# First pass of a fused attention and SwiGLU kernel: another order of weight steps, transposes and loads around the tiles of four head pairs

## The chip, the cores and the metric

The kernel runs on one core of one Trainium2 chip. The metric is the device time of one execution in microseconds (us). TensorE (PE) multiplies, VectorE (DVE), ScalarE (ACT) and GpSimd (POOL) do the elementwise work, SyncE (SP) issues DMAs. Each engine takes its instructions in the order in which the program gives them to it; between engines they wait on semaphores.

## What is computed

```python
scores = q @ k.T / sqrt(64)                    # 8 batches, 8 heads, 576 tokens, head_dim 64
p = exp(scores - rowmax) where scores >= rowmax - tau, else 0
x = (p / p.sum()) @ v                          # heads side by side: 4608 tokens x 512
g, val = x @ w_gate, x @ w_val                 # 512 -> 1536
out = (g * sigmoid(g) * val) @ w_out           # 1536 -> 512
```

q, k and v are float32. The weights arrive as 64-bit floats, and the kernel makes float32 numbers of them itself, out of the upper and the lower 32-bit word of each.

## The kernel before, in words

Heads go in pairs: a pair fills 128 partitions. The **first pass** (about the first 124 us) does batch 0, whose four pairs go by 128-token tiles. Everything behind it, seven more batches with the feed-forward block of the batch before them between, is laid out by a planner with costs of its own (`class Plan`), and is not touched.

The first pass is a loop over eight segments n, and in each over tiles x; `(n, x)` names one turn of the loop. Segments 0 to 3 are pairs 0 to 3 with tiles 0 and 1; segments 4 to 7 are pairs 3, 0, 1, 2 with tiles 2, 3 and 4 (tile 4 is half as tall). A turn gives the engines, in this order:

1. PE: the scores of this tile (L505, L513 for tile 4), for head 0 into one PSUM tile and for head 1 into another. There are two such PSUM tiles in all, so the scores of a head wait until the mask of the tile before has read them.
2. DVE: a maximum for each head (L497). Then the point `maxima`.
3. PE: attention times v of the tile before last (L609, L611), then the transposes of the tile before (L578, L582; L576, L584 from segment 4 on).
4. ACT: threshold and exponential for each head (L528, L529), then the copies of what PE has just made (L614, L585, L592). Then the point `flipped`.
5. DVE: the mask with its row sum for each head (L532), then L534 and L535. Then the point `masked`.
6. ACT: in segments 0 to 3 two small matrices with 1/sum on the diagonal (L548), which the transposes of the next turn multiply by. From segment 4 on ACT and POOL scale the tile itself instead (L542, L540). Then the point `end`.

At the four points a table written by hand, `STEPS`, says what else is issued. Its words:

- `weights 2`: fetch up to two of the 24 weight steps, w0, w1, ... (L344, on SP; 768 KB in two DMAs, from `w_gate` and from `w_val`). There are four landing places in turn; a fetch is left out if its place is still held by a step that has not been joined.
- `split`: ACT takes the upper words (L360); POOL (segments 0 to 3, L362) or ACT (later, L364) takes the lower ones; POOL clamps the upper part (L353). In segments 0 to 3 the clamp is issued with the split; later it is put off until step 5 of a turn, where `clamp_split()` issues whatever is unclamped.
- `shift`: DVE (L383), behind the clamp. `join`: DVE adds the sign (L390), then POOL adds the lower part (L400).
- `prepare`: DVE transposes the next pair's keys and queries (L738, L742). `turn`: DVE transposes a pair's other queries (L797). `scale`: POOL scales queries (L440). `qk`, `rest`, `v`: SP issues the loads of a pair's keys and queries (8 DMAs), of its other queries (4), of its values (4).

From segment 4 on a turn has regular steps besides: behind `maxima` a join; at `flipped` a split and two fetches; behind the masks, after the table's own words, a join if something is shifted, `clamp_split()`, an addition of lower parts, and a shift if a step was split in an earlier turn. There PE also fills in products of the feed-forward block (L625), which need the weights joined; ACT reads them by L640 and L641, DVE by L649, and POOL multiplies at the turn's end (L656).

`STARTS` lists the loads that SP gets ahead of the loop. Lines 750 to 752 prepare the first pair of batch 1, whose loads (`qk` at `(4, 0)`) are 8 DMAs of SP and whose queries POOL scales at `(4, 1)`.

Of the kernel before, what the change touches and what calls it, by code (L numbers as in the profile page):

```python
# [27 lines left out]
class Plan:  # L28
# [94 lines left out]

STARTS = ("weights", "v", "weights", "qk", "weights", "v", "v", "weights")

STEPS = {
    (0, 0, "flipped"): ("qk",),
    (0, 1, "maxima"): ("prepare",),  # L130
    (0, 1, "masked"): ("split",),
    (0, 1, "end"): ("scale",),
    (1, 0, "flipped"): ("split", "shift"),
    (1, 0, "masked"): ("join",),
    (1, 1, "flipped"): ("weights 2", "prepare"),
    (1, 1, "masked"): ("split", "shift"),
    (1, 1, "end"): ("join",),
    (2, 0, "maxima"): ("rest", "weights 2"),
    (2, 0, "flipped"): ("rest",),
    (2, 0, "masked"): ("shift", "scale", "split", "join"),  # L140
    (2, 0, "end"): ("weights 2",),
    (2, 1, "maxima"): ("scale", "prepare", "v", "rest"),
    (2, 1, "flipped"): ("rest", "split"),
    (3, 0, "flipped"): ("shift",),
    (3, 0, "end"): ("join",),
    (3, 1, "maxima"): ("shift", "split", "turn last"),
    (3, 1, "flipped"): ("weights 2", "scale", "prepare"),
    (3, 1, "masked"): ("split",),
    (3, 1, "end"): ("turn", "shift", "scale"),
    (4, 0, "flipped"): ("turn", "qk"),  # L150
    (4, 1, "maxima"): ("scale",),
    (4, 1, "masked"): ("scale",),
    (4, 2, "end"): ("turn",),
# [4 lines left out]
def kernel(  # L158
# [620 lines left out]
    def start(what):  # L779
        if what == "weights":  # L780
            fetch_weights()
        elif what == "v":
            load_v(unloaded.popleft())
        elif what == "qk":
            fetch_qk(unfetched.popleft())
        else:
            rest_load()

    for what in STARTS:
        start(what)  # L790
# [1980 lines left out]
```

## Time and profile before

| what | us |
|---|---|
| median of 3 runs | 1332.68 (1331.83 to 1333.17) |
| the profiled execution | 1332.23 |
| its span, first to last instruction | 1330.4 |
| PE busy in the span | 1320.2 (99%) |
| DVE, ACT, POOL busy | 1092.4, 892.9, 951.1 |
| first pass, start to the first scores of the planned part | 123.54 |
| scores of `(1,0)`, `(1,1)`, `(2,0)`, `(2,1)` begin | 15.24, 20.71, 25.48, 30.74 |
| scores of `(3,0)`, `(3,1)`, `(4,0)`, `(4,1)` begin | 36.04, 41.52, 46.29, 56.44 |

Times in the text are counted from the span's start. A busy PE is not a PE at its peak: matmuls of the two heads use different halves of the array and run beside each other when both may start, and one behind the other when the second must wait.

In rows of the timeline the columns are start, length, engine (SPq is SP's queue, PEld the weight loads), line, operation, what it writes and reads, how many, and in brackets how long the engine sat idle before and what ended it. A row of several instructions runs from the first one's start to the last one's end.

### The profile page before, as it was taken

What the parts mean: (1) busy time and instruction counts of PE and PEld (TensorE: products, weight loads), DVE (VectorE), ACT (ScalarE), POOL (GpSimd) and SP (SyncE); (2) the same over time, 40 slices, a digit from 0 to 9 for tenths busy, and PEclk for the clock granted to TensorE, in tenths of its full rate; (3) what the DMA queues carried; (4) which work ended last, traced back from release to release, by engine and by line L of the source; (5) the groups of instructions that cost most, each with busy time, mean ns of one, the idle gap of its engine ahead of it and who ended that gap; (6) DMA issues with size and microseconds to landing.
All of it is one profiled execution on the core that took longest, in us unless ns stands there. A gap on an engine that the chain in (4) does not pass through costs nothing.

```text
span 1330.4 us, 41756 instructions
## 1 busy us (share of the span) xinstructions
PE 1320.2 (99%) x16294; PEld 1119.1 (84%) x16294; DVE 1092.4 (82%) x2900; ACT 892.9 (67%) x2336; POOL 951.1 (71%) x1137
## 2 busy tenths in 40 slices
PE   8999999999999999999999999999999999999998
PEld 7777777777788878888888888887888889999998
DVE  7799988878887788878888887888788888767986
ACT  6898877677755777787777777777777775444300
POOL 3788597565695979756995779677975798866720
PEclk9999999999999999999999999999999999999999
DMA  8853334456647544656265746655465627465341
GB/s 178 220 180 108 71 81 120 126 155 178 161 168 228 168 152 114 202 157 222 71 203 165 235 107 193 180 166 154 111 202 157 217 74 227 152 208 189 96 171 40
DMA packets 230884, 209.81 MB, mean 158 GB/s; under 512 B 167968, under 2 KB 185376, under 8 KB 223008
## 3 DMA queue, kind: packets, MB, share of 16 engines
q1 hardware_dynamic: 226768, 206.22, 52.4%
q8 instruction: 129, 2.11, 0.7%
q10 hardware_dynamic: 3920, 0.92, 0.3%
q14 instruction: 67, 0.55, 0.1%
HBM read 169.08 MB, written 38.01 MB: 156 GB/s over the span
## 4 chain that ended last, share of the span: by engine, by line
PE 94%; ACT 3%; DMA 1%; POOL 1%; DVE 1%; SPq 1%; issue 0%; ACTq 0%; DVEq 0%
PE pb L1190 14%; PE px L1820 12%; PE sc L2111 10%; PE pa L1190 10%; PE xa L2211 10%; PE pe L1190 6%; PE po L1498 6%; PE sc L2601 5%; PE py L1820 4%; PE pe L1385 3%; PE pb L2601 2%; PE pg L1423 2%; PE pa L2601 2%; PE pv L1423 2%; PE py L1829 2%; PE sc L1820 1%
## 5 line engine op out<-in xcount | busy, mean ns | idle before, releaser
L2159 DVE SCALAR_TENSOR_TENSOR pall<-sc,th,pall 128x288 f32<-128x288 f32 x504 | 244.2, 514 | 39.3 <-ACT pall L2157 20.2
L2157 ACT ACTIVATE pall<-sc,nm 128x288 f32<-128x288 f32 x504 | 232.7, 497 | 34.9 <-DVE pall L2159 34.7
L1190 PE MATMUL pb<-xall,big 128*128 128x256 f32 x864 | 205.9, 381 | 0.0
L2189 DVE STREAM_TRANSPOSE pall<-pall 128x576 f32<-128x576 f32 x252 | 188.4, 764 | 19.2 <-ACT pall L2187 9.4
L971 POOL TENSOR_TENSOR big<-big 128x128 f32<-128x128 f32 (+3 forms) x226 | 167.1, 748 | 43.5 <-ACT big L1325 21.7
L2187 ACT ACTIVATE pall<-pall,ri 128x288 f32<-128x288 f32 x380 | 175.8, 527 | 27.3 <-DVE ri L2175 26.3
L1190 PEld LDWEIGHTS pb<-xall,big 128*128 128x128 f32 x864 | 161.0, 190 | 24.1 <-issue 2.2
L971 POOL TENSOR_TENSOR hall<-hall,tmp 128x512 f32<-128x512 f32 x80 | 102.1, 1278 | 87.9 <-DVE hall L1249 66.9
L2132 DVE TENSOR_REDUCE mx<-sc 128x2 f32<-128x576 f32 x168 | 125.5, 747 | 45.2 <-PE sc L2111 45.1
L2111 PE MATMUL sc<-kT,qT 64*32 64x288 f32 (+1 forms) x5376 | 144.5, 345 | 0.0
L1190 PE MATMUL pa<-xall,big 128*128 128x256 f32 x576 | 137.6, 382 | 0.0
L2111 PEld LDWEIGHTS sc<-kT,qT 64*32 64x32 f32 x5376 | 95.3, 106 | 48.3 <-issue 8.3
L2211 PE MATMUL xa<-pall,vall 64*32 64x288 f32 x4032 | 128.7, 404 | 0.0
L1190 PEld LDWEIGHTS pa<-xall,big 128*128 128x128 f32 x576 | 107.9, 190 | 17.3 <-issue 2.2
L2211 PEld LDWEIGHTS xa<-pall,vall 64*32 64x32 f32 x4032 | 74.0, 107 | 46.9 <-issue 4.0
L2184 POOL TENSOR_SCALAR pall<-pall,ri 128x288 f32<-128x288 f32 x124 | 63.5, 523 | 49.0 <-DVE ri L2175 46.9
L2168 ACT COPY sums<-sums 32x6 f32<-32x6 f32 x336 | 66.6, 198 | 31.3 <-DVE pall L2159 26.2
L1190 PE MATMUL pe<-xall,big 128*128 128x256 f32 x352 | 83.9, 381 | 0.0
L2134 DVE TENSOR_REDUCE mx<-sc 128x1 f32<-128x288 f32 x168 | 75.0, 447 | 0.0
L1190 PEld LDWEIGHTS pe<-xall,big 128*128 128x128 f32 x352 | 66.3, 190 | 10.3 <-ACT xlast L2223 0.7
L971 POOL TENSOR_TENSOR hall<-hall 128x384 f32<-128x384 f32 (+2 forms) x69 | 70.3, 1032 | 0.8
L971 POOL TENSOR_TENSOR big<-hall 128x384 f32<-128x384 f32 (+2 forms) x69 | 65.6, 972 | 4.3 <-PE pa L1190 4.2
(402 smaller groups left out, 3055.7 us busy)
## 6 DMA issues: line engine op xcount, KB each, us to landing
big<-sums_hbm SPq DMA_DIRECT2D x30, 1280.0 KB, 7.6
big<-sums_hbm SPq DMA_DIRECT2D x30, 1024.0 KB, 7.4
vall<-in_v_dram SPq DMA_DIRECT2D x112, 144.0 KB, 4.0
big<-sums_hbm SPq DMA_DIRECT2D x54, 256.0 KB, 3.6
sums_hbm<-big SPq DMA_DIRECT2D x36, 256.0 KB, 3.6
out_dram<-big SPq DMA_DIRECT2D x32, 256.0 KB, 3.1
qT<-in_q_dram SPq DMA_DIRECT2D x112, 72.0 KB, 4.2
kT<-in_k_dram SPq DMA_DIRECT2D x112, 72.0 KB, 3.0
```

The source lines that it names most:

```text
L971: nc.gpsimd.tensor_tensor(out=out, in0=a, in1=b, op=op)
L1190: nc.tensor.matmul(ps[:, i], w[:, k_, i * P:(i + 1) * P], x[:, k_, :], start=first and i == k_ == 0, stop=True, skip_group_check=True)
L1498: nc.tensor.matmul(ps, h(f), w[:, f, :], start=(f == 0), stop=(f == NF2 - 1))
L1820: nc.tensor.matmul(ps, a[:, f, :], ws[n][:, f, :], start=bank_ not in begun, stop=True, skip_group_check=True)
L2111: nc.tensor.matmul(pss[h][(slice(g * G, (g + 1) * G), *part)], qT[hs, col:col + G], kT[hs, c * SH + keys[0]:c * SH + keys[1]], start=True, ...
L2132: rs.append(job("DVE", 0.72, lambda n=n, tile_=tile_: nc.vector.tensor_reduce(out=mx[:, n:n + 2, 0], in_=tile_[:, :, 0:SH], axis=AX.X, op= ...
L2157: ej = job("ACT", 0.42, lambda x=x, n=n: nc.scalar.activation(ps[x], scs[x], AF.Exp, bias=nm[:, n:n + 1]), ej, masks.get((h, u - 1)), rank=0)
L2159: masks[x] = job("DVE", 0.45, lambda x=x, n=n: nc.vector.scalar_tensor_tensor(out=ps[x], in0=scs[x], scalar=th[:, n:n + 1], in1=ps[x], op0 ...
L2187: scaled.append(job("ACT", 0.46, lambda x=x, n=n: nc.scalar.activation(x, x, AF.Copy, scale=ri[:, n:n + 1]), rj, rank=rank))
L2189: seg["turned"].append(job("DVE", 0.72, lambda both=both: nc.vector.transpose(out=both, in_=both), *scaled, rank=rank))
L2211: nc.tensor.matmul(holds[a].ap()[x * G:(x + 1) * G, 0:SH].rearrange("d (i q) -> d i q", q=G), vr[rs, h, j, ds], p[rs, h, :, j, :], start=( ...
L2601: nc.tensor.matmul(both.ap(b_)[:, at_ * P:(at_ + 1) * P], ws[x], xd[x], start=b_ not in begun, stop=True, skip_group_check=True)
```

## The change

Only the two tables differ. Nothing is added to the computation and nothing left out; all 24 weight steps are made.

- `STARTS`: the keys and queries of the fourth pair are loaded behind pair 1's values and ahead of pair 2's; before, they came at `(0, 0)`, behind step w3.
- `prepare` of pairs 2 and 3 goes from in front of the masks of `(1, 1)` and `(2, 1)` to behind the masks of `(1, 0)` and `(2, 0)`.
- Joins: w0 goes from behind the masks of `(1, 0)` to behind those of `(1, 1)`, w1 from the end of `(1, 1)` to behind the masks of `(2, 1)`, w2 from `(2, 0)` to the end of `(3, 0)`. The shifts of w1 and w2 go to `flipped` of `(2, 0)` and `(3, 0)`.
- One split, shift and join fewer by the end of segment 3, where the next step is w6 and not w7. The end of `(4, 0)` makes that up: a join (w5), up to two fetches, a shift (w6) and a split (w7).
- As places come free later, the fetches move too: w4 to the end of `(1, 1)`, w5 to the end of `(2, 1)`, behind the loads `rest`, `v`, `rest`, `rest` of segment 2; w6 to `(3, 1)`; w7 and w8 to `(4, 0)`, w8 behind the 8 DMAs of `qk`.
- The third pair's `scale` (of pair 3's early queries) goes from `(2, 0)` to the end of `(1, 1)`.

From `(4, 1)` on the table is the same, and both orders work on the same weight step.

```diff
-STARTS = ("weights", "v", "weights", "qk", "weights", "v", "v", "weights")
+STARTS = ("weights", "v", "weights", "qk", "weights", "v", "qk", "v", "weights")
 STEPS = {
-    (0, 0, "flipped"): ("qk",),
...
-    (1, 0, "flipped"): ("split", "shift"),
-    (1, 0, "masked"): ("join",),
-    (1, 1, "flipped"): ("weights 2", "prepare"),
-    (1, 1, "masked"): ("split", "shift"),
-    (1, 1, "end"): ("join",),
-    (2, 0, "maxima"): ("rest", "weights 2"),
-    (2, 0, "flipped"): ("rest",),
-    (2, 0, "masked"): ("shift", "scale", "split", "join"),
-    (2, 0, "end"): ("weights 2",),
-    (2, 1, "maxima"): ("scale", "prepare", "v", "rest"),
-    (2, 1, "flipped"): ("rest", "split"),
+    (1, 0, "flipped"): ("split", "shift",),
+    (1, 0, "masked"): ("prepare",),
+    (1, 1, "masked"): ("split", "join",),
+    (1, 1, "end"): ("weights 2", "scale",),
+    (2, 0, "maxima"): ("rest",),
+    (2, 0, "flipped"): ("rest", "shift",),
+    (2, 0, "masked"): ("prepare",),
+    (2, 1, "maxima"): ("scale", "v", "rest",),
+    (2, 1, "flipped"): ("rest", "split",),
+    (2, 1, "masked"): ("join",),
+    (2, 1, "end"): ("weights 2",),
     (3, 0, "flipped"): ("shift",),
     (3, 0, "end"): ("join",),
-    (3, 1, "maxima"): ("shift", "split", "turn last"),
-    (3, 1, "flipped"): ("weights 2", "scale", "prepare"),
+    (3, 1, "maxima"): ("shift", "split", "turn last",),
+    (3, 1, "flipped"): ("weights 2", "scale", "prepare",),
     (3, 1, "masked"): ("split",),
-    (3, 1, "end"): ("turn", "shift", "scale"),
-    (4, 0, "flipped"): ("turn", "qk"),
+    (3, 1, "end"): ("turn", "shift", "scale",),
+    (4, 0, "flipped"): ("turn", "qk",),
+    (4, 0, "end"): ("join", "weights 2", "shift", "split",),
     (4, 1, "maxima"): ("scale",),
     (4, 1, "masked"): ("scale",),
```

## The prediction

> **What bounds the kernel now.** I read the page, then the chain of waits, then a table of stretches for the first pass, then each engine's timeline.
>
> ```profile
> span 1330.4 us, 41756 instructions
> ...
> PE 94%; ACT 3%; DMA 1%; POOL 1%; DVE 1%; SPq 1%; issue 0%; ACTq 0%; DVEq 0%
> ```
>
> PE sets the end nearly everywhere, but the chain's pieces before 124 us also run through ACT, POOL and DVE. All that the change moves lies there, so only that part is worked out; the planned part behind it keeps its order and should begin, and end, later or earlier by the same amount.
>
> One turn each, from its scores to the next scores; columns: length, then busy time of PE, PEld, DVE, ACT, POOL, clock, DMA.
>
> ```profile
> 20.71:25.48 4.77, 4.77 (x48) 3.84 (x46) 4.12 (x8) 4.45 (x12) 3.32 (x3) 1.00 0.80 186
> 25.48:30.74 5.26, 5.26 (x48) 4.24 (x46) 4.83 (x11) 4.28 (x12) 3.44 (x3) 1.00 0.94 208
> ```
>
> The same 48 matmuls take 4.77 or 5.26. The surplus is in the scores: 1.25 when both heads run beside each other, up to 1.95 when the second waits for its PSUM tile, that is, for the mask of the turn before. The turns from 15.24 to 46.29 take 5.47, 4.77, 5.26, 5.30, 5.48, 4.77: above 4.77 they lose 0.70 + 0 + 0.49 + 0.53 + 0.71 + 0 = **2.43 us**. That is all there is to win up to 46.29.
>
> Why the masks are late is in DVE's timeline:
>
> ```profile
> 23.32 0.77 DVE L738 STREAM_TRANSPOSE pall<-extra 128x576 f32<-128x576 f32 x1
> 24.01 0.40 DVE L742 STREAM_TRANSPOSE qT<-extra 128x256 f32<-128x256 f32 x1
> 24.34 0.78 DVE L532 SCALAR_TENSOR_TENSOR pall<-sc,th,pall 128x576 f32<-128x576 f32 x1
> ...
> 26.17 0.54 DVE L383 TENSOR_SCALAR big<-big 128x768 uint32<-128x768 uint32 x1
> 26.75 0.96 DVE L390 SCALAR_TENSOR_TENSOR big<-wo,big 128x768 uint32<-128x768 uint32 x1
> 27.62 1.42 DVE L497 TENSOR_REDUCE nm<-sc 128x1 f32<-128x576 f32 x2
> ```
>
> `prepare` holds DVE for 1.02 (23.32 to 24.34), although the exponential was done at 23.70. A shift and a join behind the masks hold it for 1.45 (26.17 to 27.62). Between L535 and the next maximum DVE has some 1.1 (a maximum starts about 1.27 after its scores), so one of `prepare` (1.02) or join (0.96) fits there, and not join and shift together.
>
> **The change, up to 46.29.** The 0.70 of (1,0) stays: its cause is the `prepare` in front of (0,1)'s masks, which isn't moved. At (1,1) the second exponential ends at 24.51, so the masks can end at about 25.3 in place of 25.85, and the scores at 25.48 go side by side: 0.49 won. At (2,0) a shift (0.47) goes in front of the masks, `prepare` behind: the masks end some 0.1 late. At (2,1) and (3,0) only a join or a shift is left beside the masks; of 0.53 + 0.71 about 0.1 to 0.5 stays, the larger figure if w2's join meets w1's addition on POOL (a join took 0.96 alone and 2.04 at 70.95, beside POOL's gate product). So (4,0) begins 1.2 to 1.6 earlier; I take **1.4**. The moved `prepare` of pair 3 needs its keys by about 31: their loads are issued from 20.7 to about 24 now and land by 29 even at the 4.7 that such loads took. A weight step's work less by then is no gain of its own: it comes back at the end of (4,0), where DVE sits idle for 3.64 before 57.71, ACT for 1.89 before 58.48 and POOL for 2.23 before 60.15. The extra join and shift (0.95 + 0.5 of DVE), the split (0.82 + 0.93 of ACT) and the addition (1.82 of POOL) fit, the last two with little left.
>
> **What eats the gain: w5's landing.**
>
> ```profile
> 42.76 4.35 SPq L436 DMA_DIRECT2D extra<-in_q_dram x8
> ...
> 46.72 0.94 ACT L360 ACTIVATE big<-wo 128x768 f32<-128x768 f32 x1
> 47.55 0.69 ACT L548 ACTIVATE pall<-pall,ri 128x128 f32<-128x128 f32 x2
> ...
> 49.29 1.95 PE L578 MATMUL tp<-pall 128*128 128x128 f32 x16
> ```
>
> SP issues almost without a pause up to 47. The split at (3,1) `masked` is w6 now, issued at 38.56. In the change it is w5, and its fetch stands behind the loads of segment 2, the last of which end at 47.1 today. Take away what w5 and w6 cost SP ahead of them (0.89 + 0.87, and SP's waits of 1.2 and up to 0.9 for `w_val` landings in its waits): w5 is issued at about 43.3. Its second half follows 0.45 later; these took 4.8 to land in the median, all halves 3.2 at least. So w5 is there at 47.0 to 48.9, and I take **47.9**. ACT comes to the split at 46.72 - 1.4 = 45.3 and waits; behind it on ACT stand L548, which the next transposes need, and the exponentials of (4,0). 47.9, plus 0.82 of split, plus 0.4 of the first L548 and some 0.2 of signals, lets PE's transposes start at about 49.3, and now they start at 49.29. **The gain of 1.4 is gone**; it is between 0.9 kept and 1.0 lost at the ends of the landing. On POOL the same landing holds w5's lower part and clamp, and with them `scale` (1,1) and one `turn`: by 50.5, as now.
>
> **What is new: a clamp behind a scale.** At (4,0) w7's split now comes at `end`, after that turn's `clamp_split()`. Its clamp is issued at (4,1) behind `scale` (4,0), and the shift of w7 behind it stands in front of the maximum of (4,2).
>
> ```profile
> 56.48 0.83 POOL L353 TENSOR_SCALAR big<-big 128x768 f32<-128x768 f32 x1
> ...
> 61.88 0.54 DVE L383 TENSOR_SCALAR big<-big 128x768 uint32<-128x768 uint32 x1
> 62.13 0.90 POOL L540 TENSOR_SCALAR pall<-pall,ri 128x576 f32<-128x576 f32 x1 [0.16 <-DVE ri L535]
> 62.33 0.75 DVE L497 TENSOR_REDUCE nm<-sc 128x1 f32<-128x576 f32 x1
> ...
> 63.00 1.55 POOL L440 TENSOR_SCALAR qT<-qT,scl 128x576 f32<-128x576 f32 x1
> ...
> 64.94 0.78 ACT L529 ACTIVATE pall<-sc,nm 128x576 f32<-128x576 f32 x1
> ...
> 73.87 2.06 PE L505 MATMUL sc<-pall 64*128 64x288 f32 x10 [0.85 <-DVE pall L532]
> ```
>
> Today w7's clamp is done at 57.3. Then: POOL's L440 from 63.03. It took 1.55 beside DVE's join; DVE would be waiting, so I take 0.90, L540's time for the same shape: 63.93. Clamp 0.83: 64.8. Shift 0.46, maximum 0.75, threshold 0.25: the exponential of (4,2) starts at 66.25 in place of 64.94, **+1.3** (+1.95 if L440 keeps its 1.55, +1.0 if it takes 0.6). From there the chain of waits has been ACT to 67.68, POOL's clamp of w9, DVE, and PE's scores at 73.87 behind an idle 0.85, with no slack in it, so the 1.3 passes on.
>
> The Trainium skill (SBUF — State Buffer, "SBUF: two separate sides") says that a GpSimd operation and a DVE one with two SBUF inputs exclude each other for a whole instruction. By it the 1.55 of L440 is the join's 0.95 from 63.00, and 0.60 of its own: the sum would be 0.3 lower than mine.
>
> w8 comes behind the 8 DMAs of `qk`, on the place in SP's queue that w9 has now (58.27, less 1.4), and lands at 61.1 to 62.1; ACT asks for it at 61.2. A wait of up to 1.0 there hides in the 1.3, since ACT would otherwise wait for the maximum.
>
> **Sum.** -1.4 won, +1.4 given back to w5, +1.3 for the clamp: **+1.3 us**; 1333.5 on the profiled execution's 1332.23 (span 1330.4 and 1.8 around it). The runs' median is 1332.68, 0.45 above that execution, and a new median is to be compared with it: **1334.0**.
>
> **Rivals.** A measurement of this kernel tells about 0.2% (2.7 us) from no change: faster is below 1330.0, slower above 1335.35.
>
> - *Forecast*, 1334.0 (1333.1 to 1335.0 over the landings above): 0.52.
> - *The gain stays and nothing is given back*: w5 lands by 45.5, since SP's issue alone (0.45 to 0.5 a DMA, 42 from 17.5) would allow it at 39 to 40, and the wait for the clamp finds slack that the chain doesn't show. 1332.68 - 1.4 = 1331.3; at most 2.43, were (1,0) to gain too. For it: the waits that the chain names are inferred. Against it: issues of 1.4 to 2.0 occur in SP's row whenever many loads are out. 0.20, of which 0.04 below 1330.0.
> - *One of the two only*: the gain is eaten, but the clamp's wait is hidden, or the reverse; 1332.7. 0.10.
> - *Slower*: w5 lands much later. Behind the same 8 loads of `rest`, the fetch that follows now took 1.58 to issue its first half (47.28); with that, and the 6.6 that the slowest half took, w5 lands at about 50, ACT holds L548 and the transposes 2.1 longer than I reckon, and the time is 1336.0. It decides above a landing of 49.2. 0.18, of which 0.13 above 1335.35.
>
> Range: 1331.3 to 1335.9, which leaves out about half of the second case and a third of the last. Faster 0.04, within 0.2% 0.82, slower 0.14 (0.13 and the forecast's upper edge).
>
> **What would show it.** Scores of (2,0) and (2,1) of 1.2 to 1.3 and (4,0) starting at 44.7 to 45.1: the front gain. An idle ACT ahead of L360 at 45 to 48, ended by a DMA from `w_val`, and transposes at 49 to 50: w5. DVE idle some 2.9 ahead of L383 near 62, ended by POOL L353: the clamp. Scores of (5,1), now 73.87, near 75.2, and the planned part, now 123.54, near 124.8. It would be wrong if ACT doesn't wait at L360, if L353 of w7 ran before L440, or if the planned part changed its length.

## The result, and the profile after

| | before | after |
|---|---|---|
| median, us | 1332.39 (6 runs, 1331.49 to 1333.17) | 1337.85 (6 runs, 1337.12 to 1339.44) |
| profiled execution, us | 1332.23 | 1338.06 |
| its span, us | 1330.4 | 1336.3 |
| scores of `(3,1)`, `(4,0)`, `(4,1)` begin | 41.52, 46.29, 56.44 | 40.86, 45.63, 57.65 |
| scores of `(4,2)`, `(5,0)`, `(5,1)` begin | 61.03, 66.73, 73.87 | 65.06, 70.77, 79.69 |

The change makes the kernel slower: ratio 1.0041, 95% interval 1.0029 to 1.0054, that is 5.5 us. Forecast were +1.3 us and a range up to 1335.9. (A ratio here and below can differ a little from the quotient of the two medians.)

The profiled execution after starts its first scores 0.22 sooner (6.78 against 7.00). With this as the first step, the way to the 5.82 at the scores of `(5,1)` is: -0.22 of start, -0.44 up to `(4,0)`, +1.87 from there to `(4,1)`, +2.6 at the maximum of `(4,1)`, +2.0 at that of `(4,2)` (the last two counted at the exponentials behind these maxima). The first two places are read from the timeline of after:

```profile
27.49 1.81 POOL L400 TENSOR_TENSOR big<-big,extra 128x768 uint32<-128x768 uint32 x1
27.88 1.85 DVE L383 TENSOR_SCALAR big<-big 128x768 uint32<-128x768 uint32 x1
29.65 0.80 DVE L532 SCALAR_TENSOR_TENSOR pall<-sc,th,pall 128x576 f32<-128x576 f32 x1
...
41.39 4.63 POOL L400 TENSOR_TENSOR big<-big 128x768 uint32<-128x768 uint32 x2
...
44.80 0.42 SPq L344 DMA_DIRECT2D wo<-in_moe_w_val_dram  x1
...
47.98 0.53 POOL L440 TENSOR_SCALAR hall<-hall,scl 128x320 f32<-128x320 f32 x1
48.55 0.51 DVE L797 STREAM_TRANSPOSE pall<-hall 128x320 f32<-128x320 f32 x1 [1.95 <-DMA wo<-in_moe_w_val_dram]
48.78 0.90 ACT L360 ACTIVATE big<-wo 128x768 f32<-128x768 f32 x1 [2.59 <-DMA wo<-in_moe_w_val_dram]
...
50.02 2.05 PE L578 MATMUL tp<-pall 128*128 128x128 f32 x16 [0.91 <-ACT pall L548]
```

w1's shift (L383), in front of the masks of `(2,0)`, takes 1.85; the shift at 61.88 in the kernel before took 0.54. It begins 0.39 after POOL has begun w0's addition (L400) and ends 0.43 after the addition ends at 29.30. The masks (L532), whose exponential was there at 28.3, start at 29.65, and the scores of `(2,1)` run one behind the other (5.47 for the turn, the kernel before 5.30). Then w5: its second half is issued at 44.80, ACT sits idle for 2.59 in front of its split, and PE's transposes of `(4,0)` come at 50.02 and not at 49.29.

Another wait lies beside that one. The maximum of `(4,0)` comes at 50.09, 4.46 after its scores (1.90 in the kernel before, 48.19 after 46.29), and the exponential waits for it until 50.86, though ACT was free again at 50.41. Ahead of the maximum stands the `turn` of pair 0 (L797). Its bracket names a DMA, but it transposes what POOL's `scale` (L440) has written, and starts 0.04 after that ends at 48.51. POOL comes late to this scale because the additions of w1 and w2 fill it until 46.02; they stand behind the `scale` for `(3,1)`, which waited for its queries until 38.86.

The next two places, again in the timeline of after (idle time ahead of an instruction, and what ended it, in the brackets):

```profile
52.44 1.82 POOL L400 TENSOR_TENSOR big<-big,extra 128x768 uint32<-128x768 uint32 x1 [0.97 <-DVE big L390]
54.80 1.68 POOL L540 TENSOR_SCALAR pall<-pall,ri 128x576 f32<-128x576 f32 x1 [0.54 <-PE xa L609]
56.44 2.52 POOL L400 TENSOR_TENSOR big<-big 128x768 uint32<-128x768 uint32 x1
59.06 0.83 POOL L353 TENSOR_SCALAR big<-big 128x768 f32<-128x768 f32 x1
59.85 1.81 POOL L400 TENSOR_TENSOR big<-big 128x768 uint32<-128x768 uint32 x1
59.92 2.15 DVE L383 TENSOR_SCALAR big<-big 128x768 uint32<-128x768 uint32 x1 [2.64 <-POOL big L353]
62.00 1.41 DVE L497 TENSOR_REDUCE nm<-sc 128x1 f32<-128x576 f32 x2
...
67.03 0.75 POOL L440 TENSOR_SCALAR qT<-qT,scl 128x576 f32<-128x576 f32 x1
67.86 1.62 POOL L353 TENSOR_SCALAR big<-big 128x768 f32<-128x768 f32 x2
68.72 1.17 DVE L383 TENSOR_SCALAR big<-big 128x768 uint32<-128x768 uint32 x1 [2.59 <-POOL big L353]
69.82 0.74 DVE L497 TENSOR_REDUCE nm<-sc 128x1 f32<-128x576 f32 x1
```

The upper part is the catch-up at the end of `(4,0)`. Its shift of w6 stands in DVE's row in front of the maximum of `(4,1)`. w6's clamp (59.06) stands in POOL's row behind w3's addition, a scaling of the tile and w4's addition, which fill POOL from 52.44 on but for a pause of 0.54. So DVE waits 2.64 with the scores of `(4,1)` ready since about 58.9, and then the shift itself takes 2.15, beside w5's addition. The maximum (L497) comes at 62.00, 4.35 after the scores of its turn began; in the kernel before it was 1.27 (57.71 after 56.44). The lower part is the second wait, one turn on: w7's clamp behind `scale` (L440), the shift behind the clamp, the maximum of `(4,2)` behind the shift.

From `(5,1)` on nothing more of note is added (5.82 there, 5.9 at the end of the span).

### The profile page after: what moved, and what is told of

The parts are those of the page before. It is cut to its first block, busy times and chain, and to the rows that moved or that the text cites. A ratio compares the mean times of both kernels' runs of the same rounds, so it can differ in the third digit from the quotient of the medians.

```text
span 1336.3 us, 41751 instructions
## 1 busy us (share of the span) xinstructions
PE 1321.0 (99%) x16294; PEld 1119.1 (84%) x16294; DVE 1096.2 (82%) x2900; ACT 894.3 (67%) x2337; POOL 949.5 (71%) x1136
## 4 chain that ended last, share of the span: by engine, by line
PE 92%; ACT 2%; DMA 2%; DVE 1%; POOL 1%; SPq 1%; issue 1%; ACTq 0%; DVEq 0%; POOLq 0%
PE pb L1190 14%; PE px L1820 12%; PE sc L2111 10%; PE pa L1190 10%; PE xa L2211 9%; PE pe L1190 6%; PE po L1498 6%; PE sc L2601 5%; PE py L1820 4%; PE pe L1385 3%; PE pb L2601 2%; PE pg L1423 2%; PE pa L2601 2%; PE pv L1423 2%; PE py L1829 2%; PE sc L1820 1%
## 5 line engine op out<-in xcount | busy, mean ns | idle before, releaser
L971 POOL TENSOR_TENSOR big<-big 128x128 f32<-128x128 f32 (+3 forms) x226 | 167.1, 748 | 43.6 <-ACT big L1325 21.8
```

The lines of the kernel that those rows point to most:

```text
L971: nc.gpsimd.tensor_tensor(out=out, in0=a, in1=b, op=op)
```

## The experiments

The theories. A: the loss comes from the catch-up, whose shifts wait for clamps in front of two maxima and run beside POOL's additions; w5's landing and the shift in front of `(2,0)`'s masks only eat the gain of the front. Its rival puts the loss ahead of `(4,1)`, to w5's landing and to POOL's row of work. All times below are medians; a ratio is against the kernel before, run beside it.

**The catch-up left out.** The change without its line at the end of `(4,0)`; one weight step more is left to the planned part.

```diff
-    (4, 0, "end"): ("join", "weights 2", "shift", "split",),
```

> The changed kernel without the four steps at the end of (4,0): nothing is made up there, every later weight step comes one place later in the first pass, and one step more is left to the planned part. Theory A (two shifts stand in front of two maxima and wait for their clamps: w6's in front of (4,1), 2.6 us, w7's in front of (4,2), 2.0 us): both waits go, the maxima of (4,1) come about 1.3 after their scores, and the time is 1333 to 1334 (1337.85 less 4 to 4.6, perhaps something back for the step left over). Theory B (POOL and ACT are late as such, because of w5's landing and the pile of additions behind it, and the shifts only show it): at least 3 of the 5.5 us stay, 1335.5 or more.

Measured: 1333.27 us, ratio 1.0006 (0.9997 to 1.0016), so 4.6 us are back. In the timeline of DVE no shift is left in front of the maximum of `(4,1)`, which waits for its scores:

```profile
54.25 0.55 DVE L383 TENSOR_SCALAR big<-big 128x768 uint32<-128x768 uint32 x1
57.94 1.42 DVE L497 TENSOR_REDUCE nm<-sc 128x1 f32<-128x576 f32 x2 [3.13 <-PE sc L505]
```

It comes 1.28 after the scores (56.66). The order of the front is that of the change, but in this execution the queries and w5 landed sooner (ACT went on at 47.75), and the scores of `(4,1)` come 1.0 sooner. Behind them the comparison is clean: from the scores of `(4,1)` to those of `(5,1)` it takes 17.44, as in the kernel before (17.43), and 22.04 in the change. These 4.6 arise behind `(4,1)`, where the rival has nothing.

**w7's clamp ahead of the scale.** The change, with `clamp_split()` added to the catch-up, so that w7's clamp no longer stands behind POOL's `scale`.

```diff
-    (4, 0, "end"): ("join", "weights 2", "shift", "split",),
+    (4, 0, "end"): ("join", "weights 2", "shift", "split", "clamp",),
```

> The changed kernel with w7's clamp issued right behind its split at the end of (4,0), ahead of the scales of (4,1). Theory A: DVE's shift of w7 no longer waits near 68; the maximum of (4,2) comes 2 us sooner, and the time is about 1335.9. The wait in front of (4,1) stays. Theory B: POOL is the limit, and one instruction moved on it changes less than 0.5 us: 1337.4 or more.

Measured: 1336.0 us, ratio 1.0027 (1.0017 to 1.0037): 1.85 less than the change. The shift of w7 takes 0.54 and waits for nothing (65.15), the maximum of `(4,2)` comes 4.5 after that of `(4,1)` (4.6 in the kernel before, 7.8 in the change). The wait for w6's clamp stays as it was (2.64, and 2.15 for the shift), though here too w5 landed sooner (ACT went on at 47.97) and the maximum of `(4,0)` comes 1.94 after its scores: that wait does not hang on a late front.

**The catch-up without its shift.** The join of w5, the fetches and w7's split stay at the end of `(4,0)`; w6 is shifted behind the masks of `(4,1)`.

```diff
-    (4, 0, "end"): ("join", "weights 2", "shift", "split",),
+    (4, 0, "end"): ("join", "weights 2", "split",),
```

> The change, with the shift of w6 left out of the line at the end of (4, 0); the join of w5, the fetches and the split of w7 stay there, and w6 is shifted in its regular place, behind the masks of (4, 1). Theory: the cost of the catch-up is the place of its shift, in front of the maxima of (4, 1) and so, one turn on, of (4, 2): the maximum of (4, 1) comes 1.3 after its scores, no shift waits for a clamp, and most of the 4.6 us comes back; left may be up to 1.5 for w7's split on ACT in front of the exponential of (4, 1): 1333.2 to 1334.9 us. Rival, that the work itself is too much for ACT and POOL at (4, 0): 1336.0 to 1338.0 us.

Measured: 1334.33 us, ratio 1.0020 (1.0011 to 1.0028). So some 3.5 of the 4.6 hang on the place of one instruction of 0.54, which takes the place of the next one, w7's shift, along. The maximum of `(4,1)` comes at 57.95, 1.27 after its scores, and the exponential at 59.40, as without the catch-up. The other 1.1 is not w7's split in front of that exponential, as the expectation had it. By the timeline it is the step behind it, w8: its split comes a turn sooner than without the catch-up, and ACT sits idle for 1.26 in front of it (62.84), ended by a DMA from `w_val`. The exponential of `(4,2)` comes at 66.56 (65.1 without the catch-up). No run tests this last reading.

**w1's shift in front of other masks.** The change, with w1's shift at `(1,1)`, where POOL makes no addition (`join one` joins a single step, so that w1 isn't joined with w0).

```diff
-    (1, 1, "masked"): ("split", "join",),
+    (1, 1, "flipped"): ("shift",), (1, 1, "masked"): ("split", "join one",),
...
-    (2, 0, "flipped"): ("rest", "shift",),
+    (2, 0, "flipped"): ("rest",),
```

> The changed kernel with w1's shift moved from (2,0), where it ran 1.85 us beside POOL's addition of w0, to in front of the masks of (1,1), where POOL adds nothing (the join at (1,1) is still w0's alone). If a shift is held by an addition on POOL, it takes 0.55 there, the scores of (2,1) and (3,0) run side by side and (3,1) starts 0.6 to 1.0 sooner, at about 40.0. If the shift is slow for another reason (a wait for the clamp, its place in the program), it stays over 1.5. Either way the time is within 0.5 of 1337.85, since ACT waits for w5 at 48.8 whatever comes before.

Measured: 1336.32 us, ratio 1.0027 (1.0017 to 1.0038), 1.5 less than the change. The shift (23.16) takes 0.98. It again ends 0.41 after a POOL instruction, the lower part of w2 (22.83, 0.90 long). The front gain is then there: scores of `(4,0)` at 44.83, 1.3 sooner than before when counted from `(1,0)`. On the time the expectation was missed: more of the gain passes `(4,1)` than it said. But in this profiled execution w5's second half let ACT go on at 47.51, not at 48.78, and POOL came to its additions 0.8 sooner; how much of the 1.5 is the shift's place and how much an earlier landing is not shown.

**w5 fetched sooner.** The change, with the fetch of w5 ahead of pair 3's values and of two loads of other queries.

```diff
-    (2, 1, "maxima"): ("scale", "v", "rest",),
-    (2, 1, "flipped"): ("rest", "split",),
-    (2, 1, "masked"): ("join",),
-    (2, 1, "end"): ("weights 2",),
+    (2, 1, "maxima"): ("scale",),
+    (2, 1, "flipped"): ("split",),
+    (2, 1, "masked"): ("join", "weights 2", "v", "rest", "rest",),
```

> The changed kernel with w5 fetched ahead of pair 3's values and the last two loads of queries, at about 37.3, so that it lands by 43. Theory A: ACT's wait of 2.6 ahead of w5's split goes and the transposes of (4,0) start at 48 to 49, but POOL comes to w5's lower part at 48.5 anyway, for the additions of w1 and w2 and w4's parts stand before it, so w6's clamp is only some 0.4 sooner and both shift waits stay: 1337 or a little more. Theory B (w5's landing is the root): everything behind it moves up by the 2 to 3 us, to 1335 or less.

Measured: 1336.81 us, ratio 1.0032 (1.0021 to 1.0044). That is 1.0 less than the change by the medians, but the six runs of each overlap (1335.79 to 1338.48 and 1337.12 to 1339.44), so a gain is not shown. ACT no longer waits for w5 (split at 46.07), and the transposes of `(4,0)` come at 48.95 against 50.02. Yet the scores of `(4,1)` begin at 57.26 against 57.65 and its maximum comes at 61.6 against 62.0, 0.4 sooner, as the first theory said. The reason is the wait beside it: the `turn` (L797) starts at 48.55 as in the change, here with POOL's L440 named for its 1.95 of idle time, the maximum of `(4,0)` comes at 49.70, and ACT sits idle for 1.05 until it has come. With w5 there in time, POOL's row holds `(4,1)` back nearly as long as both did.

**Can the front gain be kept at all?** Four kernels without the catch-up, each with one edit more: w1's shift at `(1,1)`; besides it w5 fetched ahead of two loads of other queries; besides these POOL's `scale` for `(3,1)` at the end of `(2,1)`; and besides these w1's addition ahead of w3's lower part and clamp in POOL's row.

The diff is the last one's, against the change; `split upper` is ACT's part of a split, `split lower` POOL's lower part and clamp.

```diff
-    (1, 1, "masked"): ("split", "join",),
+    (1, 1, "flipped"): ("shift",), (1, 1, "masked"): ("split", "join one",),
...
-    (2, 0, "flipped"): ("rest", "shift",),
+    (2, 0, "flipped"): ("rest",),
...
-    (2, 1, "maxima"): ("scale", "v", "rest",),
-    (2, 1, "flipped"): ("rest", "split",),
-    (2, 1, "masked"): ("join",),
-    (2, 1, "end"): ("weights 2",),
+    (2, 1, "maxima"): ("v",),
+    (2, 1, "flipped"): ("split upper",),
+    (2, 1, "masked"): ("join", "split lower", "weights 2", "rest", "rest",),
+    (2, 1, "end"): ("scale",),
...
-    (4, 0, "end"): ("join", "weights 2", "shift", "split",),
```

> The change without the line at the end of (4, 0), and with w1's shift at (1, 1) in front of the masks, where POOL makes no addition of 768 columns. Theory A (the catch-up costs some 4.6 us and the shift at (2, 0) some 0.7 of the front gain): the shift takes 0.55 to 0.9, scores (3, 1) begin at about 40.0 and (4, 0) at about 44.8, w5 still lands at 47.5 to 48.7 and ACT waits for it, so little of the front gain is left: 1332.3 to 1333.0 us (without the catch-up alone it was 1333.27). Rival (the front gain passes whole): 1331.3 or less.

> As the run before, and w5 fetched ahead of two of segment 2's loads of other queries. Theory A, that w5's landing is what eats the front gain: w5 is there by about 45, ACT doesn't wait for it, transposes of (4, 0) at about 48.0 to 48.3, and 1.2 to 1.6 of gain are kept: 1331.0 to 1332.0 us, and scores (5, 1) at about 72.6. Rival, that POOL's row of work (scale (3, 1) waiting for the late loads of other queries, the additions of w1 and w2 behind it, then scale (0, 1), the turn of pair 0 on DVE and only then the maximum of (4, 0)) holds as much: maximum of (4, 0) still at 48.2 or later, 1332.2 to 1333.0 us.

> As the run before, and the scale that POOL makes for the second tile of (3, 1) comes at the end of (2, 1), not at its maxima. If POOL's row of work holds the maximum of (4, 0), the maximum comes about 1 us sooner than in the run before and the time is 0.5 to 1.0 lower; if w5 was all, the two are alike within 0.4 us.

> As the run with the late scale, and at (2, 1) POOL gets w1's addition ahead of w3's lower part and clamp (ACT's part of w3's split stays where it was). Theory: what keeps the front gain from the fifth segment is POOL's additions, which fall on DVE's shifts and joins. With w1's addition at about 36.5 to 38.4, over the maxima of (3, 0), the shift of w2 is held by 0.5 at most, the maximum of (3, 1) comes at 41.4 to 41.9 (42.3 to 42.8 in the three runs before), scores (4, 0) at 44.8 to 45.4 and the time is 1331.4 to 1332.3 us. Rival, that something behind (4, 0) holds as much (ACT or POOL there): scores (4, 0) sooner, (4, 1) not, 1332.6 to 1333.3 us.

The gain over the kernel before, in us, at the scores of four turns, each counted from the scores of `(1,0)`:

| | time, us | ratio | `(3,1)` | `(4,0)` | `(4,1)` | `(5,2)` |
|---|---|---|---|---|---|---|
| w1's shift moved | 1332.88 | 0.9997 (0.9988 to 1.0006) | 1.31 | 0.19 | -0.71 | -0.70 |
| and w5 sooner | 1332.91 | 1.0004 (0.9995 to 1.0012) | 1.30 | 0.81 | 0.47 | 0.48 |
| and scale later | 1333.62 | 1.0006 (0.9997 to 1.0014) | 0.75 | 0.05 | -0.26 | -0.13 |
| and addition first | 1332.67 | 1.0002 (0.9993 to 1.0011) | 1.32 | 0.76 | 0.42 | 0.43 |

(The gains are those of the profiled executions. That of the first was the slowest of its eleven, 1335.05. That of the second reached `(1,0)` 1.0 later than the others, 16.18 against 15.1, and yet its time is that of the median; what the other executions do is not shown.)

The first row: the gain is there at `(3,1)`, and then w2's join takes 1.50 beside w1's addition, the maximum of `(3,1)` comes at 42.28, 2.23 after its scores, and at `(4,0)` ACT waits 2.57 for w5. So of the 2.0 lost between `(3,1)` and `(4,1)`, 1.1 is gone ahead of `(4,0)`, where w5 has no part. The second row: ACT doesn't wait for w5 any more, 1.2 of the 2.0 are back at `(4,1)`, the join still takes 1.47, and half a microsecond is kept; the 1.2 to 1.6 expected if w5 were all are not there. In the third the scale no longer holds w1's addition back, which now (37.52) falls on w2's shift (37.90, and 1.85 long); its time was expected 0.5 to 1.0 lower than the second row's, or alike, and is 0.7 higher by the medians. In the fourth it lies over the maxima of `(3,0)`, which read PSUM, and those take no longer for it:

```profile
36.48 1.81 POOL L400 TENSOR_TENSOR big<-big 128x768 uint32<-128x768 uint32 x1 [6.58 <-DVE big L390]
36.48 1.42 DVE L497 TENSOR_REDUCE nm<-sc 128x1 f32<-128x576 f32 x2
```

There the maximum of `(3,1)` comes at 41.35, as expected, and w2's join takes 0.94. But w2's addition now lies over w3's shift (42.69, and 1.35 long), and 0.4 is left at `(4,1)` and `(5,2)`. The time is still that of the kernel before; 1331.4 to 1332.3 was expected. Against the trace of before, these four, the one without the catch-up and the one without its shift, which all end the first pass one step behind, each lose 0.27 near 177 us and 0.57 near 936 us, in the planned part. (The profiled executions of the first and the fourth lose another 1.1 and 0.7 near 262 us, where PE sits idle without a wait that the profile shows; no other run has that, and what it comes from is not known.) In the run without the catch-up:

```profile
936.50 1.58 PE L1820 MATMUL px<-wo,hall 128*128 128x128 f32 x12 [0.61 <-DVE hall L1249]
```

In the kernel before, this L1820 starts at 935.81 with no idle time ahead of it.

**The step made up later.** The fourth kernel, with the catch-up at the end of `(7,2)`.

```diff
-    (4, 2, "end"): ("turn",),
+    (4, 2, "end"): ("turn",), (7, 2, "end"): ("join", "weights 2", "shift", "split",),
```

> As the run with w1's addition first, with the catch-up (join, fetches, shift, split) at the end of (7, 2), the last turn of the first pass. Theory: in the planned part every kernel with one step less pays 0.27 at 177 us and 0.57 at 936 us, which the kernels with the step made up don't; made up at the end of the first pass, where the planned part has other work for PE, it saves 0.84 and costs less: 1331.5 to 1332.2 us, and no jumps at 177 and 936. Rival: it costs there as much or more, since ACT's split of 1.9 comes in front of the first exponential of the planned part: 1332.7 to 1334.0 us.

Measured: 1336.37 us, ratio 1.0031 (1.0019 to 1.0044): worse than either theory said. In front of the first maximum of the planned part stand the shift and a join, long ones again (1.63 and 2.46), and PE runs out of work:

```profile
136.27 1.16 PE L2111 MATMUL sc<-kT,qT 64*32 64x288 f32 x9 [2.55 <-DVE pall L2159]
```

The jump at 177 us is gone, so that one goes with the missing step. The one near 936 us is still there (0.57); what it hangs on stays open. The six kernels that end the first pass one step behind have it, and this one; the change and all the others that make the step up at `(4,0)` or keep the order of before do not.

**Two single parts of the change, on the kernel before.** The order of the first loads alone:

```diff
-STARTS = ("weights", "v", "weights", "qk", "weights", "v", "v", "weights")
+STARTS = ("weights", "v", "weights", "qk", "weights", "v", "qk", "v", "weights")
-    (0, 0, "flipped"): ("qk",),
```

> The kernel before with one edit alone: the fourth pair's keys and queries are loaded where the change loads them. Nothing waits for them there before 33 us, so both theories: within 0.5 us of the kernel before. Were it slower by 0.7 or more, the order of the loads at the start would be a cost that neither theory has.

Measured: 1332.49 us, ratio 0.9998 (0.9989 to 1.0006): worth nothing, as expected. (In its profiled execution the scores of `(5,2)` come at 80.99, 0.87 later than in that of the kernel before, and yet the span is 1330.7 against 1330.4: not all of a delay in the first pass need show at the end.) And `prepare` alone, behind the masks, with all weight steps where they were:

```diff
-    (1, 0, "masked"): ("join",),
-    (1, 1, "flipped"): ("weights 2", "prepare"),
+    (1, 0, "masked"): ("join", "prepare"),
+    (1, 1, "flipped"): ("weights 2",),
...
-    (1, 1, "end"): ("join",),
+    (1, 1, "end"): ("join", "scale"),
-    (2, 0, "masked"): ("shift", "scale", "split", "join"),
+    (2, 0, "masked"): ("shift", "split", "join", "prepare"),
-    (2, 1, "maxima"): ("scale", "prepare", "v", "rest"),
+    (2, 1, "maxima"): ("scale", "v", "rest"),
```

> The kernel before, with the preparing of pairs 2 and 3 moved behind the masks of (1, 0) and (2, 0) as in the change, and every weight step left where it was. Theory: behind a turn's masks DVE has room for one of the two, so a join and a preparing of 1.0 each make the next maximum some 0.9 late, and what is won in front of the masks is lost there: scores (4, 0) within 0.5 of the kernel before, 1332.2 to 1333.2 us. Rival, that the preparing in front of the masks was the cost by itself: scores (4, 0) 0.5 to 1.2 sooner and 1331.3 to 1332.0 us.

Measured: 1332.25 us, ratio 1.0001 (0.9992 to 1.0010). The maximum of `(1,1)` comes at 22.3 (22.0 before, 21.8 in the change), that of `(2,1)` at 33.6 (32.8, 32.6), and the scores of `(4,0)` at 46.61. So the moves of `prepare` win nothing by themselves; with the weight step taken out besides they do, and that step has to be paid elsewhere. The weight step taken out alone was not run.

None of the kernels is measurably faster than the one before.

## Why the prediction was wrong

The sum was -1.4, +1.4, 0, +1.3. Measured, in the same order and place: -0.44, +1.87, +2.6, +2.0.

- **The failed step: the catch-up costed at nothing.** "The extra join and shift (0.95 + 0.5 of DVE), the split (0.82 + 0.93 of ACT) and the addition (1.82 of POOL) fit, the last two with little left." Lengths were laid against idle time, engine by engine, and they do fit so: DVE was idle for 2.64 even in the change. But the shift has a place in DVE's row, in front of the maximum of `(4,1)`, and needs a clamp that has a place in POOL's row. The prediction made just this argument for w7, one turn on, and did not make it for w6. The rows of before would have given 0.06: the clamp in that place (w7's, there) was done at 57.31, 0.40 ahead of the maximum, and a shift is 0.46. What came of it is 3.08: to the 0.06 come 0.68, since w3's join and addition followed a late maximum of `(4,0)` (0.54 with the clamp sooner, where that maximum was on time but w5's lower part came late on POOL); 0.70, since w4's addition stood still beside the extra join (2.52, and 1.82 before); and 1.65, since the shift stood still beside the extra addition. ACT had some 0.5 to spare, which leaves 2.6. So three quarters of it are pairs of instructions that the catch-up itself put side by side, and that were costed by their lengths alone. The run without the shift gives 3.5 us back, w7's wait included.
- **The front gain, 1.4 forecast, 0.44 got.** (In the profiled executions of the three other kernels with the same front, `(4,0)` came between 0.12 sooner and 0.13 later than before, counted from `(1,0)`.) The scores of `(2,0)` did start side by side, and `prepare` behind the masks did what it was to do. The 1.4 assumed 0.47 for the shift at `(2,0)`. It took 1.85 beside w0's addition; put elsewhere, `(4,0)` came 1.3 sooner. The risk was named for w2's join beside w1's addition, and at 0.5.
- **w5's landing: late as forecast, but not alone.** Forecast 47.9, and in the profiled execution ACT went on at 48.78 (47.42 to 48.67 in the five other kernels with that fetch in the same place); idle ACT ahead of L360, ended by a DMA from `w_val`, was in the list of what would show it. Transposes at 50.02, forecast 49.3. The gain was eaten, and 1.2 more at `(4,1)`. But the sum had one cause there, and the trace has two side by side: POOL's row held the maximum of `(4,0)`, and for that the prediction had nothing. With w5 fetched in time `(4,1)` came only 0.4 sooner. And the size changes from execution to execution with the landings: counted from `(1,0)`, `(4,1)` came 1.4 later than before in the change and 0.2 to 0.4 later in the three other kernels with the same front, where the `scale` for `(3,1)` had its queries at 36.4 to 37.0 and not at 38.86.
- **w7's clamp behind the scale: right mechanism, 1.3 forecast, 2.0 got.** The idle time was forecast at 2.9 and is 2.59. L440 took 0.75, between the 0.90 of the sum and the 0.6 of its lower case. The surplus is in the shift: 1.17 and not 0.46, since POOL goes on with w8's clamp. The run with the clamp ahead of the scale took away 1.85.
- "From there the chain has no slack in it, so the 1.3 passes on": right, and for the 2.6 as well. In the kernels without the catch-up the scores of `(5,2)` come 20.8 to 21.0 after the exponential of `(4,1)`, wherever that lies (59.16 to 80.12 before, 58.5 to 79.47 with the addition first).
- The slower rival had w5's landing as its cause (1336.0); the time came out past it, and the cause is another.

## What to carry to other kernels

A step that is moved into idle time costs its place before it costs its length: follow each of its instructions down the queue of its engine to what it needs there, and ask what is queued behind it while it waits. Where one such chain has been found, walk the same chain for every other instruction of the kind that the change issues. And a piece of work that is taken out of a full stretch has to be paid where it is put back: look for that place first. Where two waits lie side by side, taking one away shows only what the other leaves (0.4 for w5's landing here), so look at what the trace waits for then.

## What the runs showed of the hardware

A one-input shift of 768 columns on DVE takes 0.54 to 0.56 alone. Beside a POOL instruction that was at work when it began, it ends 0.40 to 0.43 after that instruction does, however long that is: 1.85 and 2.15 beside additions (after), 1.85 (third of the four kernels), 1.17 beside the second of two clamps, 0.98 beside a lower part. By these ends it does not run slower; it stands still until POOL is done. The reverse is there too: w4's addition in the profile after began 0.46 behind w5's join, which ended at 57.28, and took 2.52 in place of 1.82. A POOL instruction that is itself standing still beside a join does not hold the shift behind that join: in the kernel before, L540 began at 52.91, inside a join that ended at 53.61, and took 1.69 (0.90 at 62.13), and the shift at 53.52 took 0.55. Maxima of PSUM tiles took 1.42 for two with an addition beside them and without.

The Trainium skill says the same (SBUF — State Buffer, "SBUF: two separate sides"): a GpSimd instruction and a DVE instruction in a two-port mode, or a DVE instruction with two SBUF inputs where the GpSimd one reads SBUF, lock each other out for a whole instruction, and the one that starts first goes ahead. The traces agree for the join, which has two inputs (2.52 for the addition behind it). They agree for the shift too (1.85 and 2.15), if it runs in a two-port mode, which no trace here shows. The prediction had drawn on the two inputs alone, and used that for POOL's scale.
